# A scratch write cut at row 32 instead of row 22, and the last step's gate in halves

## The chip, the core and the metric

The kernel runs on one core of a Trainium2 chip. The core has TensorE (PE in the profile, with PEld for its weight loads), VectorE (DVE), ScalarE (ACT), GpSimd (POOL) and SyncE (SP), which only issues DMAs; ACT issues DMAs too. The metric is the device time of one execution in microseconds. The kernel before took 2562.18 us in the median of three runs, from 2557.64 to 2562.96. The profiled execution took 2562.1 us.

## The reference

An FFT filter along the sequence, followed by a two-layer block with the gate h·cos(h):

```python
X = np.fft.rfft(x, axis=1)                    # x: (8, 3008, 256)
Y = X * (filt_r + 1j * filt_i)[None, :, :]
y = np.fft.irfft(Y, n=3008, axis=1)           # reshaped to 24064 tokens of 256
h = y @ w_in                                  # (256, 2048)
g = h * np.cos(h)
out = g @ w_out                               # (2048, 256)
```

x and the filters are float32; the two weight matrices arrive as float64.

## The kernel before

The length 3008 = 47·64 is transformed with small matrix products. A batch goes through stage 1 (47 points), stages 2 and 3 (64 points forward, filter, 64 points back) and stage 4 (47 points back). Between the stages the data lie in scratch tensors in device memory: z1 after stage 1, z2 after stage 3. Stage 4 works by **units** of five columns of 47 points each (the third has one, the last two have three); it loads a unit from z2 (line 425), multiplies it (line 435) and writes the split result y (lines 442 to 452). A **chunk** is 512 tokens, and there are 47; the first chunk needs units 0 to 2, which cover rows 0 to 21 of a batch's part of z2 when two rows of 24 values are counted per column.

The block runs over **steps** (c, s): chunk c, and slice s of eight slices of the 2048 hidden values, 376 steps in all. `hidden` makes 12 matmuls into a two-bank tile `hp` (line 466), `gate` turns it into h·cos(h), split into a high part `gh` and a low part `gl` (lines 476 to 483), and `project`, which runs two steps later, makes 12 matmuls into two accumulators (line 495). After slice 7 each accumulator is scaled on ACT and written out (lines 503 and 504). `hp` has two buffers, so step k+2 waits until the gate of step k has read its tile. Matrices and data in products of this kind are kept as a high and a low part and multiplied three times.

The first batch has its own code. `first23` writes each of its 12 pieces of z2 (128 rows of 2 KB) in two DMAs: the first n0 rows at once from ACT (line 409), which is all that the first chunk waits for, and the rest later from SP (line 412). n0 is twice the first column that chunk 0 doesn't need, 22, so that the two DMAs carry 22 and 106 rows.

The weights are loaded as pairs of 32-bit words and converted on the chip (`prep_w`, lines 222 to 239): a DMA from SP into one of three `raw` buffers, two operations on ACT, a shift on DVE (line 234), an addition on POOL, and the split on ACT and POOL. Sixteen such pieces exist, called w_in and w_out 0 to 7 in what follows; nine are converted before the steps begin, and the other seven among the steps of chunk 0. A scheduler puts each engine's instructions into one fixed order per engine, guided by its own estimate of the time of each instruction; SP's DMAs are issued in their fixed order too, and each engine waits at an instruction until what it needs is there.

Of the kernel before, what the change touches and what calls it, by code (L numbers as in the profile page):

```python
# [10 lines left out]
F32 = mybir.dt.float32  # L11
F32R = mybir.dt.float32r
I32 = mybir.dt.int32
AF = mybir.ActivationFunctionType
ALU = mybir.AluOpType
# [6 lines left out]
P = 128  # L22
NJ = NB // 2
TJ = 2 * NA
TC = 512
NC = B * S // TC
NDT = D // P
NFT = DFF // P
TWO_PI = 2.0 * math.pi
# [109 lines left out]
def _units():  # L139


    sizes = [5, 5, 1] + [5] * 99 + [3, 3]
    assert sum(sizes) == B * NB
    starts = np.concatenate([[0], np.cumsum(sizes)])
    return [(int(a), int(n)) for a, n in zip(starts, sizes)]
# [10 lines left out]
def fft_filter_then_cos_glu(ctx: ExitStack, tc: tile.TileContext, ins, outT):  # L156
    nc = tc.nc
# [35 lines left out]
    NS = NFT // 2  # L193
# [4 lines left out]
    units = _units()  # L198
# [4 lines left out]
    n_first = len(of_chunk[0])  # L203
# [57 lines left out]
    def psum_f(b):  # L261
        if b == 0 and len(done) < n_first:
            if not spare:
                spare.extend(ps_h.tile([P, 2, 512], F32, name="hp")[:, u] for u in range(2))
                spare.append(ps_f.tile([P, 512], F32, name="ps", tag="ps"))
            return spare.pop(0)
        return ps_f.tile([P, 512], F32, name="ps", tag="ps")
# [115 lines left out]
    def first23(i, fas, fbs):  # L383
        cols = slice(512 * i, 512 * i + 512)
        zf = fft.tile([P, 512], F32, name="zf", tag="ld", bufs=5)
        nc.sync.dma_start(zf, z1s[0].rearrange("j (h c k) d -> (j h c) (k d)", h=2, c=2)[:, cols])
        yield
        ps = psum_f(0)
        nc.tensor.matmul(ps, mats["f2"], zf, start=True, stop=True)
        half = slice(2 * (i % 2), 2 * (i % 2) + 2)  # L390
        ya = fft.tile([P, 512], F32, name="ya", bufs=2)
        yb = fft.tile([P, 512], F32, name="yb", tag="sw", bufs=2)
        for y, f in ((ya, fas), (yb, fbs)):
            nc.vector.tensor_tensor(y, ps, f[i // 2][:, half].rearrange("p k d -> p (k d)"), ALU.mult)
        yield
        ps = psum_f(0)
        if i == 0:
            for m, c in (("30", slice(0, D)), ("3", slice(D, 512))):
                nc.tensor.matmul(ps[:, c], mats["f" + m], ya[:, c], start=True, stop=False)
                nc.tensor.matmul(ps[:, c], mats["f" + m + "i"], yb[:, c], start=False, stop=True)  # L400
        else:
            nc.tensor.matmul(ps, mats["f3"], ya, start=True, stop=False)
            nc.tensor.matmul(ps, mats["f3i"], yb, start=False, stop=True)
        tag, bufs = at2[i]
        z = fft.tile([P, 512], F32, name="z2t", tag=tag, bufs=bufs)
        nc.scalar.copy(z, ps)
        to = z2[:NJ].rearrange("j (h c k) d -> (j h c) (k d)", h=2, c=2)[:, cols]
        n0 = 2 * units[n_first][0]
        nc.scalar.dma_start(to[:n0], z[:n0])
        yield  # L410
        wrote2.setdefault(0, []).append(i)
        nc.sync.dma_start(to[n0:], z[n0:])  # L412
# [43 lines left out]
    gs, accs = {}, {}  # L456

    def hidden(c, s):
        yh, yl = ys[c]
        assert of_chunk[c] <= done  # L460
        hp = ps_h.tile([P, 2, 512], F32, name="hp")
        for u in range(2):
            fs = slice(u * P, (u + 1) * P)
            for t in range(NDT):
                for n, (w, y) in enumerate(((0, yh), (0, yl), (1, yh))):
                    nc.tensor.matmul(hp[:, u], w_in[s][w][:, t, fs], y[:, t],  # L466
                                     start=(t == 0 and n == 0), stop=(t == NDT - 1 and n == 2))
                if u == 0 or t == 0:
                    yield
        with tc.high_priority() if c == 0 else nullcontext():  # L470
            gs[c, s] = gate(hp)

    def gate(h):

        g = moe.tile([P, 2, TC], F32, name="g")
        nc.vector.tensor_scalar(g, h, 0.25, MAGIC, ALU.add, ALU.add)  # L476
        nc.vector.scalar_tensor_tensor(g, g, MAGIC, h, ALU.subtract, ALU.subtract)  # L477
        nc.scalar.activation(g, g, AF.Sin, bias=half_pi, scale=-TWO_PI)  # L478
        nc.vector.tensor_tensor(g, g, h, ALU.mult)  # L479
        gh = moe.tile([P, 2, TC], F32R, name="gh")  # L480
        nc.scalar.copy(gh, g)  # L481
        gl = moe.tile([P, 2, TC], F32R, name="gl")
        nc.gpsimd.tensor_tensor(gl, g, gh.bitcast(F32), ALU.subtract)  # L483
        return gh, gl

    def project(c, s):
        if s == 0:
            accs[c] = [ps_o.tile([P, 512], F32, name=f"acc{e}") for e in range(2)]
        gh, gl = gs.pop((c, s))
        for e in range(2):  # L490
            acc = accs[c][e]
            es = slice(e * P, (e + 1) * P)
            for u in range(2):
                for n, (w, g) in enumerate(((0, gh), (1, gh), (0, gl))):
                    nc.tensor.matmul(acc, w_out[s][w][:, u, es], g[:, u],  # L495
                                     start=(s == 0 and u == 0 and n == 0),
                                     stop=(s == NFT // 2 - 1 and u == 1 and n == 2))
                if e == 0 or u == 0:
                    yield
        if s == NFT // 2 - 1:  # L500
            for e in range(2):
                o = moe.tile([P, TC], F32, name="o")
                nc.scalar.activation(o, accs[c][e], AF.Copy, scale=TWO_PI)
                nc.scalar.dma_start(outT[e * P : (e + 1) * P, TC * c : TC * (c + 1)], o)
            del accs[c], ys[c]


# [17 lines left out]
    with tc.tile_pool(name="first", bufs=12) as first, tc.manual_schedule(engines={mybir.EngineType.SP}):  # L525
        fas, fbs, load, sign = filters(first)
        ones = [first1(i, first) for i in range(NJ // 4)]
        twos = [first23(i, fas, fbs) for i in range(n23)]
        for g in ones:
            next(g)  # L530
# [6 lines left out]
        for what in "fzzfzzfzfzzfzzfwzwzwzwwww":  # L537
# [5 lines left out]
            else:  # L543
                g = prep.pop(0)(first if len(raws) < 4 else None)
# [15 lines left out]
    moe = ctx.enter_context(tc.tile_pool(name="moe", bufs=2, reuse_waits="tile"))  # L560
# [23 lines left out]
    last = [-1000]  # L584
# [20 lines left out]
    for b in range(1, B):  # L605
# [5 lines left out]
        for i in range(n1):  # L611
            t = start + step * (2 * i + 1)
            plan(stage1(b, i), t - AHEAD1, [t, t + step])
        for i in range(n23):
            t = start + step * (2 * n1 + 2 * i + 2) + GAP12
# [6 lines left out]
    for k in range(len(steps) + LAG):  # L622
        parts = []
        if k < len(steps):
            c, s = steps[k]
            if c == 0:
                while prep and len(prep) > 2 * (NS - 1 - s) - JUST_W:
                    convert()
            parts.append(hidden(c, s))
        if k >= LAG:  # L630
            parts.append(project(*steps[k - LAG]))
        now = SLOTS * k
        for g in parts:
            for _ in range(SLOTS // 2):
                run_due(now)
                next(g, None)
                now += 1
# [52 lines left out]
```

## Time and profile before

| | |
|---|---|
| median of three runs | 2562.18 us |
| profiled execution | 2562.1 us |
| its span, first to last instruction | 2560.3 us |
| PE busy | 2455.7 us, 96% |
| DVE, ACT, POOL busy | 74%, 50%, 56% |
| mean granted clock of TensorE | 0.979 |

All times inside the execution count from the start of the span. What lies outside the span is 1.8 us. A row of the timeline or of a group names the engine, the line of the program, the operation, what is written from what, and the busy time. A queue's row (SPq, ACTq) is the issue of a DMA, not its transfer. "DMA share" is the mean busy share of the core's 16 DMA engines. The bracket behind a row, or the part behind the second bar, is the time for which the engine stood idle before it, and the instruction or DMA that ended it.

### The profile page before, as it was taken

To read this page: it belongs to the slowest core of one execution; us is meant where nothing else is said; L and a number is where in the kernel's file an instruction comes from. 1 tells how busy PE (TensorE), PEld (TensorE's weight loads), DVE (VectorE), ACT (ScalarE), POOL (GpSimd) and SP (SyncE) were. 2 spreads that over 40 slices of the span, in tenths; PEclk is the share of its full clock that TensorE was granted. 3 is DMA by queue.
4 is the path that set the end of the run, shared out by engine and by line. 5 is a ranking of instruction groups with operands and counts; after the bars stand their busy time and mean duration, and the time that the engine had idled before them with its cause. 6 is when DMAs were issued, how large, how long until landed. Compare 5 with 4: busy or idle time off the path is not lost.

```text
span 2560.3 us, 29873 instructions
## 1 busy us (share of the span) xinstructions
PE 2455.7 (96%) x10783; PEld 1967.7 (77%) x10783; DVE 1885.4 (74%) x1911; ACT 1286.1 (50%) x1707; POOL 1430.5 (56%) x826
## 2 busy tenths in 40 slices
PE   7369889999999999999999999999999999999999
PEld 2257767888888888888888888888888888888887
DVE  2177987888678877888668886787768886666665
ACT  1355564555545555555545555455554554444443
POOL 1366664656656565656546665566555554444443
PEclk8679999999999999999999999999999999999999
DMA  9253342322322232222313223222312211000000
GB/s 318 72 166 89 129 144 65 119 82 82 85 83 91 90 91 71 93 90 78 93 47 105 86 85 85 79 94 74 100 43 88 99 54 48 24 21 9 17 9 17
DMA packets 134749, 212.27 MB, mean 83 GB/s; under 512 B 12521, under 2 KB 64281, under 8 KB 134601
## 3 DMA queue, kind: packets, MB, share of 16 engines
q1 hardware_dynamic: 82385, 137.97, 17.7%
q10 hardware_dynamic: 52216, 72.39, 8.8%
q8 instruction: 86, 1.41, 0.2%
q14 instruction: 62, 0.51, 0.1%
HBM read 135.33 MB, written 74.97 MB: 82 GB/s over the span
## 4 chain that ended last, share of the span: by engine, by line
PE 82%; DVE 7%; DMA 3%; issue 3%; SPq 2%; ACT 2%; POOL 1%; POOLq 0%; ACTq 0%; DVEq 0%
PE hp L466 36%; PE acc L495 36%; PE ps L435 3%; PE ps L251 2%; PE ps L252 2%; PE ps L253 2%; SPq L412 2%; DVE g L476 1%; DMA xf<-in_x 1%; DVE sw L325 1%; DVE g L477 1%; DMA raw<-in_w_in 1%; ACT g L478 1%; DVE g L479 1%; DVE xo L280 1%
## 5 line engine op out<-in xcount | busy, mean ns | idle before, releaser
L483 POOL TENSOR_TENSOR gl<-g,gh 128x1024 fp32r<-128x1024 f32 x376 | 910.7, 2422 | 825.6 <-ACT gh L481 510.7
L466 PE MATMUL hp<-y,w_in 128*128 128x512 f32 x4512 | 1132.6, 400 | 65.8 <-DVE g L479 63.8
L466 PEld LDWEIGHTS hp<-y,w_in 128*128 128x128 f32 x4512 | 845.3, 190 | 266.6 <-issue 59.8
L495 PE MATMUL acc<-gh,w_out 128*128 128x512 f32 x3008 | 896.9, 396 | 0.7 <-ACT gh L481 0.7
L479 DVE TENSOR_TENSOR g<-g,hp 128x1024 f32<-128x1024 f32 x376 | 457.9, 1218 | 320.6 <-ACT g L478 320.1
L478 ACT ACTIVATE g<-g,half_pi 128x1024 f32<-128x1024 f32 x376 | 433.4, 1153 | 484.2 <-DVE g L477 436.6
L495 PEld LDWEIGHTS acc<-gh,w_out 128*128 128x128 f32 x3008 | 564.0, 188 | 131.1 <-ACT gh L481 1.1
L481 ACT CAST gh<-g 128x1024 fp32r<-128x1024 f32 x376 | 394.9, 1051 | 430.5 <-DVE g L479 424.1
L476 DVE TENSOR_SCALAR g<-hp 128x1024 f32<-128x1024 f32 x376 | 458.8, 1220 | 137.7 <-PE hp L466 130.3
L495 PE MATMUL acc<-gl,w_out 128*128 128x512 f32 x1504 | 549.9, 400 | 1.3 <-POOL gl L483 1.3
L477 DVE SCALAR_TENSOR_TENSOR g<-g,hp 128x1024 f32<-128x1024 f32 x376 | 458.0, 1218 | 9.9
L495 PEld LDWEIGHTS acc<-gl,w_out 128*128 128x128 f32 x1504 | 283.7, 189 | 66.7 <-POOL gl L483 2.1
L452 POOL TENSOR_TENSOR y<-y,y 128x470 fp32r<-128x470 f32 (+29 forms) x142 | 124.9, 884 | 55.8 <-ACT y L449 55.8
L435 PEld LDWEIGHTS ps<-m,z 120*128 120x128 f32 (+1 forms) x816 | 129.3, 192 | 21.0
L314 POOL TENSOR_TENSOR zl<-zf,zh 128x512 fp32r<-128x512 f32 x84 | 111.7, 1330 | 47.8 <-DVE zh L313 24.5
L331 POOL TENSOR_TENSOR yl<-ya,yh 128x512 fp32r<-128x512 f32 x84 | 113.2, 1348 | 42.1 <-ACT yh L330 42.0
L435 PE MATMUL ps<-m,z 120*128 120x120 f32 (+1 forms) x816 | 129.2, 273 | 0.0
L325 DVE SCALAR_TENSOR_TENSOR sw<-sw,sg,f 128x256 f32<-128x256 f32 x168 | 116.9, 735 | 0.0
L313 DVE CAST zh<-zf 128x512 fp32r<-128x512 f32 x84 | 93.1, 1108 | 23.1 <-DMA zf<-z 13.4
L327 DVE TENSOR_TENSOR ya<-ya,sw 128x512 f32<-128x512 f32 x84 | 98.5, 1173 | 0.0
L330 ACT CAST yh<-ya 128x512 fp32r<-128x512 f32 x84 | 51.8, 618 | 91.0 <-DVE ya L327 90.7
L449 ACT CAST y<-y 128x470 fp32r<-128x470 f32 (+29 forms) x150 | 66.9, 456 | 41.3 <-DVE y L443 38.9
(96 smaller groups left out, 1413.3 us busy)
## 6 DMA issues: line engine op xcount, KB each, us to landing
z<-z SPq DMA_DIRECT2D x101, 240.0 KB
out_t<-o ACTq DMA_DIRECT2D x94, 256.0 KB
f<-in_fb SPq DMA_DIRECT2D x84, 256.0 KB
f<-in_fa SPq DMA_DIRECT2D x84, 256.0 KB
zf<-z SPq DMA_DIRECT2D x84, 256.0 KB
z<-z2t ACTq DMA_DIRECT2D x84, 256.0 KB
xf<-in_x SPq DMA_DIRECT2D x42, 480.0 KB
z<-z1t ACTq DMA_DIRECT2D x84, 240.0 KB
```

The lines of the kernel that those rows point to most:

```text
L325: nc.vector.scalar_tensor_tensor(sw[:, ks], sw[:, ks], sg[:, 2 * i + k : 2 * i + k + 1], fbt[:, ks], ALU.mult, ALU.mult)
L331: nc.gpsimd.tensor_tensor(yl, ya, yh.bitcast(F32), ALU.subtract)
L435: nc.tensor.matmul(v[:, t, a * r : (a + 1) * r], zf[:, a, t * P : (t + 1) * P], mats[f"m4{a}"][:r, :r], start=True, stop=True)
L452: (nc.vector if i < 2 * n_first else nc.gpsimd).tensor_tensor(yl, part, yh.bitcast(F32), ALU.subtract)
L466: nc.tensor.matmul(hp[:, u], w_in[s][w][:, t, fs], y[:, t], start=(t == 0 and n == 0), stop=(t == NDT - 1 and n == 2))
L476: nc.vector.tensor_scalar(g, h, 0.25, MAGIC, ALU.add, ALU.add)
L477: nc.vector.scalar_tensor_tensor(g, g, MAGIC, h, ALU.subtract, ALU.subtract)
L478: nc.scalar.activation(g, g, AF.Sin, bias=half_pi, scale=-TWO_PI)
L479: nc.vector.tensor_tensor(g, g, h, ALU.mult)
L481: nc.scalar.copy(gh, g)
L483: nc.gpsimd.tensor_tensor(gl, g, gh.bitcast(F32), ALU.subtract)
L495: nc.tensor.matmul(acc, w_out[s][w][:, u, es], g[:, u], start=(s == 0 and u == 0 and n == 0), stop=(s == NFT // 2 - 1 and u == 1 and n == 2))
```

## The change

There are three edits. The first sets n0 to 32, so that a piece of the first batch is written as 32 rows from ACT and 96 rows from SP. The second concerns the last of the 376 steps alone: its gate runs as two calls on 512 columns each, one behind each half of the 12 matmuls, and the subtraction that makes `gl` is on VectorE there; the other steps keep one call on 1024 columns with the subtraction on GpSimd. For that, the tiles `g`, `gh` and `gl` are now allocated ahead of the matmuls in every step. The third concerns the last accumulator of the last chunk: columns 0 to 255 are scaled on ScalarE and written from its queue as before, and columns 256 to 511 are scaled on VectorE and written from SP's queue.

```diff
@@ first23
-        n0 = 2 * units[n_first][0]
+        n0 = 32
         nc.scalar.dma_start(to[:n0], z[:n0])
         yield
         wrote2.setdefault(0, []).append(i)
         nc.sync.dma_start(to[n0:], z[n0:])
@@ hidden, gate
+        last = (c, s) == (NC - 1, NS - 1)
+        g = moe.tile([P, 2, TC], F32, name="g")
+        gs[c, s] = gh, gl = [moe.tile([P, 2, TC], F32R, name=v) for v in ("gh", "gl")]
         for u in range(2):
...
+                if last and t == NDT - 1:
+                    gate(*(v[:, u] for v in (hp, g, gh, gl)), nc.vector)
                 if u == 0 or t == 0:
                     yield
-        with tc.high_priority() if c == 0 else nullcontext():
-            gs[c, s] = gate(hp)
+        if not last:
+            with tc.high_priority() if c == 0 else nullcontext():
+                gate(hp, g, gh, gl, nc.gpsimd)
...
-        nc.gpsimd.tensor_tensor(gl, g, gh.bitcast(F32), ALU.subtract)
-        return gh, gl
+        engine.tensor_tensor(gl, g, gh.bitcast(F32), ALU.subtract)
@@ project
-                nc.scalar.activation(o, accs[c][e], AF.Copy, scale=TWO_PI)
-                nc.scalar.dma_start(outT[e * P : (e + 1) * P, TC * c : TC * (c + 1)], o)
+                n = 2 if (c, e) == (NC - 1, 1) else 1
+                for k in range(n):
+                    cols = slice(k * TC // n, (k + 1) * TC // n)
+                    to = outT[e * P : (e + 1) * P, TC * c + cols.start : TC * c + cols.stop]
+                    if k:
+                        nc.vector.tensor_scalar(o[:, cols], accs[c][e][:, cols], TWO_PI, None, ALU.mult)
+                        nc.sync.dma_start(to, o[:, cols])
+                    else:
+                        nc.scalar.activation(o[:, cols], accs[c][e][:, cols], AF.Copy, scale=TWO_PI)
+                        nc.scalar.dma_start(to, o[:, cols])
```

The scheduler's estimates change with the first edit, and so the fixed orders differ in many places of the program. Three of them follow. The first is SP's queue where the rest of the first batch is written (z_112 is z2, z2t a piece of it in SBUF, z_619 and z_624 the tiles of units 3 and 4). Before:

```order
L222 DMA raw<-in_w_out 128x2x512
L222 DMA raw<-in_w_in 128x2x512
L412 DMA z_112<-z2t 106x512 x12
L222 DMA raw<-in_w_out 128x2x512
L306 DMA f<-in_fb 128x512
L307 DMA f<-in_fa 128x512
L306 DMA f<-in_fb 128x512
L307 DMA f<-in_fa 128x512
L306 DMA f<-in_fb 128x512
L222 DMA raw<-in_w_in 128x2x512
```

Now:

```order
L222 DMA raw<-in_w_out 128x2x512
L222 DMA raw<-in_w_in 128x2x512
L412 DMA z_112<-z2t 96x512 x12
L425 DMA z_619<-z_112 120x2x256
L222 DMA raw<-in_w_out 128x2x512
L306 DMA f<-in_fb 128x512
L307 DMA f<-in_fa 128x512
L306 DMA f<-in_fb 128x512
L307 DMA f<-in_fa 128x512
L222 DMA raw<-in_w_in 128x2x512
L306 DMA f<-in_fb 128x512
L222 DMA raw<-in_w_out 128x2x512
```

The loads of w_out 3 and w_in 4, the twelve writes, and then the loads of w_out 4 and w_in 5 stand in the same sequence; the load of unit 3 has moved up between the writes and w_out 4, and that of unit 4 follows right behind the rows shown.

The second place is PE's order between steps 1 and 2 of chunk 0 (w_in_1 belongs to step 1, w_in_2 to step 2; line 466 is now line 469). Before:

```order
L466 MATMUL hp<-y_555,w_in_1_82 128x512
L466 MATMUL hp<-y_554,w_in_1_83 128x512
L466 MATMUL hp<-y_554,w_in_2_84 128x512
L466 MATMUL hp<-y_555,w_in_2_84 128x512
L466 MATMUL hp<-y_554,w_in_2_85 128x512
```

Now:

```order
L469 MATMUL hp<-y_555,w_in_1_82 128x512
L469 MATMUL hp<-y_554,w_in_1_83 128x512
L435 MATMUL ps<-m_310,z_619 128x120
L435 MATMUL ps<-m_312,z_619 128x120
L435 MATMUL ps<-m_310,z_619 128x120
L435 MATMUL ps<-m_312,z_619 128x120
L435 MATMUL ps<-m_310,z_624 128x120
L435 MATMUL ps<-m_312,z_624 128x120
L435 MATMUL ps<-m_310,z_624 128x120
L469 MATMUL hp<-y_554,w_in_2_84 128x512
L469 MATMUL hp<-y_555,w_in_2_84 128x512
L469 MATMUL hp<-y_554,w_in_2_85 128x512
```

Seven matmuls of units 3 and 4, which followed step 2 before, now stand ahead of it.

The third place is PE's order at the end of the program (w_in_7 belongs to the last step, w_out_5 and w_out_6 to the projections of the two steps before it). Before:

```order
L466 MATMUL hp<-y_18812,w_in_7_94 128x512
L466 MATMUL hp<-y_18811,w_in_7_95 128x512
L495 MATMUL acc_19275<-gh,w_out_5_106 128x512
L495 MATMUL acc_19275<-gh,w_out_5_107 128x512
L495 MATMUL acc_19276<-gh,w_out_5_106 128x512
```

Now:

```order
L497 MATMUL acc_19275<-gh,w_out_6_108 128x512
L497 MATMUL acc_19275<-gh,w_out_6_109 128x512
L497 MATMUL acc_19276<-gh,w_out_6_108 128x512
L497 MATMUL acc_19276<-gh,w_out_6_109 128x512
L469 MATMUL hp<-y_18814,w_in_7_94 128x512
L469 MATMUL hp<-y_18815,w_in_7_94 128x512
L469 MATMUL hp<-y_18814,w_in_7_95 128x512
L469 MATMUL hp<-y_18814,w_in_7_94 128x512
L469 MATMUL hp<-y_18815,w_in_7_94 128x512
L469 MATMUL hp<-y_18814,w_in_7_95 128x512
L497 MATMUL acc_19275<-gl,w_out_6_108 128x512
```

Of the last step's 12 matmuls the first six stand where they were, ahead of the projection with w_out_5, and the last six have moved behind that projection and the first four matmuls of the next.

More of the change, by code (lines that the diff above doesn't have):

```diff
@@ L467, in hidden, with gate @@
                                      start=(t == 0 and n == 0), stop=(t == NDT - 1 and n == 2))
+                if last and t == NDT - 1:
+                    gate(*(v[:, u] for v in (hp, g, gh, gl)), nc.vector)
                 if u == 0 or t == 0:
                     yield
-        with tc.high_priority() if c == 0 else nullcontext():
-            gs[c, s] = gate(hp)
-    def gate(h):
-        g = moe.tile([P, 2, TC], F32, name="g")
+        if not last:
+            with tc.high_priority() if c == 0 else nullcontext():
+                gate(hp, g, gh, gl, nc.gpsimd)
+    def gate(h, g, gh, gl, engine):
         nc.vector.tensor_scalar(g, h, 0.25, MAGIC, ALU.add, ALU.add)
@@ L479, in gate @@
         nc.vector.tensor_tensor(g, g, h, ALU.mult)
-        gh = moe.tile([P, 2, TC], F32R, name="gh")
         nc.scalar.copy(gh, g)
-        gl = moe.tile([P, 2, TC], F32R, name="gl")
-        nc.gpsimd.tensor_tensor(gl, g, gh.bitcast(F32), ALU.subtract)
-        return gh, gl
+        engine.tensor_tensor(gl, g, gh.bitcast(F32), ALU.subtract)
     def project(c, s):
```

## The prediction

> **What bounds the kernel now.** I read the groups of the page first, then the busy times by stage, then the waits of the stage that stands out. The costliest group names PE's one long idle time:
>
> ```profile
> L466 PE MATMUL hp<-y,w_in 128*128 128x512 f32 x4512 | 1132.6, 400 | 65.8 <-DVE g L479 63.8
> ```
>
> Where it lies is seen from the busy time by stage (columns: stretch, its length, busy time of PE, PEld, DVE, ACT and POOL with counts, TensorE's granted clock, DMA share, GB/s):
>
> ```profile
> 87.00:96.00 9.00, 8.27 (x24) 6.21 (x24) 1.18 (x4) 3.88 (x8) 5.05 (x4) 0.69 0.13 51
> 96.00:137.00 41.00, 0.00 (x0) 0.00 (x0) 0.00 (x0) 0.45 (x1) 0.00 (x0) 0.54 0.29 106
> 137.00:200.00 63.00, 50.32 (x205) 39.47 (x206) 54.23 (x54) 37.38 (x59) 48.72 (x29) 0.86 0.51 139
> 200.00:330.00 130.00, 122.92 (x540) 97.86 (x539) 108.52 (x113) 70.44 (x102) 83.17 (x52) 0.97 0.37 113
> 330.00:500.00 170.00, 160.86 (x705) 128.54 (x704) 136.76 (x138) 88.25 (x123) 104.67 (x63) 0.98 0.35 104
> 500.00:2300.00 1800.00, 1798.65 (x8078) 1463.69 (x8077) 1391.62 (x1411) 948.76 (x1248) 1043.27 (x601) 1.00 0.25 78
> ```
>
> From 500 us on PE has no idle time worth a name. From 96 to 137 us no engine works at all. So whatever shortens that hole shifts everything behind it by as much, because all engines stand still in it together. The waits between 85 and 200 us (total, times, longest) give its chain:
>
> ```profile
> PE hp L466 <- DVE g L479: 51.8, 4, 48.2
> DVE t L234 <- ACT o L231: 47.4, 2, 47.0
> ACT o L231 <- DMA raw<-in_w_out: 44.6, 2, 44.1
> ```
>
> Step 2's matmuls wait for the gate of step 0 to release `hp`; that gate stands behind a weight conversion in DVE's fixed order; the conversion waits on ACT for the load of w_out 4. That load stands in SP's queue behind the twelve writes of line 412:
>
> ```profile
> 77.97 0.40 SPq L222 DMA_DIRECT2D raw<-in_w_out  x1
> 78.62 0.40 SPq L222 DMA_DIRECT2D raw<-in_w_in  x1
> 79.06 43.36 SPq L412 DMA_DIRECT2D z<-z2t  x12
> 122.52 4.30 SPq L222 DMA_DIRECT2D raw<-in_w_out  x1
> ```
>
> And while the writes run, the DMA engines are nearly empty:
>
> ```profile
> 40.00:64.00 24.00, 20.92 (x48) 8.57 (x46) 9.71 (x16) 5.08 (x9) 7.84 (x5) 1.00 1.04 395
> 83.00:122.00 39.00, 10.59 (x35) 8.20 (x33) 3.51 (x10) 5.56 (x13) 7.58 (x6) 0.59 0.13 52
> ```
>
> A share of 0.13 of 16 engines is two engines (2/16 = 0.125), at some 25 GB/s each, where the same core moved 395 GB/s from 40 to 64 us. One write of 106 rows of 2 KB is 217 kB, so at 52 GB/s it takes 4.2 us, and twelve take 50 us. The hole is 106 rows going through two engines.
>
> **Part 1: 96 rows instead of 106.** The question is over how many engines 96 rows go. The nearest row is the first batch's input, 96 rows of 2 KB, which was alone in the queue from 5 to 7 us:
>
> ```profile
> xf<-in_x SPq DMA_DIRECT2D x4, 192.0 KB
> 5.00:7.00 2.00, 2.00 (x4) 0.75 (x3) 0.69 (x1) 0.00 (x0) 0.00 (x0) 1.00 1.00 303
> ```
>
> With 96 rows the share is 1.00, at 303 GB/s. So a write of 197 kB costs between 0.50 us (at 395 GB/s) and 0.65 us (at 303), and twelve cost 6.0 to 7.8 us in place of 50.
>
> [...]
>
> What is late next? The queue's order behind 78 us is: w_out 3 and w_in 4 (1.05 MB), the twelve writes (2.36), unit 3 (0.25), w_out 4 (0.52), four filter loads (1.05), w_in 5 (0.52), a filter load (0.26), w_out 5 (0.52), unit 4 (0.25). The instructions at both ends of the hole:
>
> ```profile
> 87.29 8.27 PE L466 MATMUL hp<-y,w_in 128*128 128x512 f32 x24 [1.97 <-ACT y L449]
> 91.79 0.62 ACT L238 CAST w_in<-o 128x512 fp32r<-128x512 f32 x1 [1.26 <-POOL o L235]
> 136.55 0.66 ACT L231 ACTIVATE o<-raw 128x512 f32<-128x512 f32 x1 [44.14 <-DMA raw<-in_w_out]
> 137.66 1.22 DVE L476 TENSOR_SCALAR g<-hp 128x1024 f32<-128x1024 f32 x1
> 142.44 1.21 DVE L479 TENSOR_TENSOR g<-g,hp 128x1024 f32<-128x1024 f32 x1
> 143.80 4.58 PE L466 MATMUL hp<-y,w_in 128*128 128x512 f32 x12 [48.24 <-DVE g L479]
> ```
>
> Up to and with w_out 4 it is 4.18 MB, from about 78.5 us: 10.6 us at 395 GB/s, 13.8 at 303, so the last byte at 89.1 to 92.3. For issue and receipt I add 2.2 us (an estimate: the last output DMA, below, is issued at 2557.43 and the span ends at 2560.3; less 0.7 us for its 262 kB). W_out 4 is then there at 91.3 to 94.5. ACT is not free for it before 92.41 (91.79 + 0.62). From ACT's start to the first gate DVE took 1.11 us (136.55 to 137.66), so that gate starts at 93.5 to 95.6, and step 2, which followed 6.14 us later (137.66 to 143.80), at 99.7 to 101.7. Step 1's matmuls, done at 95.56, are early enough, since DVE turns to them 2.5 us after it begins.
>
> The moved order adds a wait of its own: matmuls of unit 4 now stand ahead of step 2, so PE can't begin step 2 before unit 4's load lands. That is 6.78 MB after 78.5 us: at 395 GB/s 95.7 + 2.2 = 97.9, at 303 GB/s 103.1. Behind it on PE stands step 2, and for that the gates of DVE. So step 2 starts at 99.7 to 103.1; I take 101, between the gate's and the load's ends: **42.8 us** earlier, with bounds 40.7 and 44.1. The seven matmuls themselves lie in PE's idle time.
>
> The ten rows more per piece that ACT writes are 12 × 20 kB = 0.25 MB, 0.6 us at 395 GB/s, spread over DMAs of 42 to 75 us while the filters and weights load. I take nothing; at worst 0.6 us.
>
> **Part 2: the last step.** The end before:
>
> ```profile
> 2541.53 2.96 PE L466 MATMUL hp<-y,w_in 128*128 128x512 f32 x12
> 2542.76 1.22 DVE L479 TENSOR_TENSOR g<-g,hp 128x1024 f32<-128x1024 f32 x1 [1.28 <-ACT g L478]
> 2544.07 1.05 ACT L481 CAST gh<-g 128x1024 fp32r<-128x1024 f32 x1 [1.34 <-DVE g L479]
> 2550.85 2.36 POOL L483 TENSOR_TENSOR gl<-g,gh 128x1024 fp32r<-128x1024 f32 x1 [3.19 <-ACT gh L481]
> 2553.26 3.52 PE acc L495 x8
> 2557.43 0.34 ACTq L504 DMA_DIRECT2D out_t<-o  x1
> ```
>
> PE waits for `gl`, then runs the last eight matmuls in 3.52 us, 0.44 each, where twelve take 2.80 (0.23 each) in the steady state. Halves cost as these groups do (the third and fourth: shortest, median and longest):
>
> ```profile
> 2538.89 2.80 PE acc L495 x12
> L394 DVE TENSOR_TENSOR ya<-ps,ff 128x512 f32<-128x512 f32 x4 | 2.8, 690 | 3.0 <-PE ps L389 3.0
> L503 ACT ACTIVATE o<-acc x94: 574/597/604, 211.2 to 2556.8; 128x512 f32<-128x512 f32 x94
> L452 DVE TENSOR_TENSOR y<-y,y x8: 164/644/1731, 83.8 to 177.8; 128x470 fp32r<-128x470 f32 x4, 128x84 fp32r<-128x84 f32 x1, 128x10 fp32r<-128x10 f32 x1, 128x74 fp32r<-128x74 f32 x1
> ```
>
> With 0.6 to 0.7 us for an operation on a half and 0.1 for a hand-over: DVE is free at 2543.98 and the first half is in `hp` by then. Two operations to 2545.3, the sine to 2546.0, the product to 2546.7, `gh` at 2547.4, `gl` on DVE at 2548.1. The second half's matmuls now run after 12 + 4 others, ending near 2541.53 + 22 × 0.233 = 2546.7 plus their own 1.4 = 2548.1, just when DVE takes them up: `gh` at 2551.7, `gl` at 2552.4. PE comes to the last projection at 2549.9, does six matmuls of the first half to 2551.3, waits 0.4, and ends at 2553.2, against 2553.26 + 3.52 = 2556.78. The longest chain is then one accumulator of 0.60 us and half of the other, 0.35, both on ACT, and their two DMAs: the last issue near 2554.4 against 2557.43. **3.0 us** gained.
>
> Bounds: if `gl`'s first half takes the 1.73 us of the longest such row, the second half slips by 1.1 us, and 1.9 are left; if the first accumulator's eviction were free too, 3.6. VectorE's half of the last accumulator ends before ACT's, and gains at most the 0.3 that ACT's second operation is shorter by.
>
> **The sum.** The profiled execution took 2562.1 us, 0.1 below the median, so it stands for it. 2562.1 − 42.8 − 3.0 = 2516.3, say **2516**. The order of everything up to 500 us has changed as well. PE was idle there for 12.7 + 7.1 + 9.1 = 28.9 us behind the hole; I allow 5 us either way for how the new order falls. Its own range: 2562.1 − 44.1 − 3.6 − 5 = 2509 to 2562.1 − 40.7 − 1.9 + 5 + 0.6 = 2525.
>
> **Rivals.**
> - *The DMA engines become the bound.* Rows of the stretch behind the hole show loads of weights and units together at a lower rate:
>
> ```profile
> 139.00:149.00 10.00, 5.20 (x20) 4.34 (x20) 6.61 (x7) 7.72 (x10) 4.95 (x4) 0.59 1.06 296
> ```
>
>  The 395 GB/s of 40 to 64 us speak against it. If the queue made only 200 GB/s, unit 4 would land at 78.5 + 33.9 + 2.2 = 114.6, step 2 would gain 29, and the time would be 2530. It decides from below 330 GB/s, where the load and not the gate is last.
> - *The new order costs more than I allow.* Half of the 28.9 us idle time again, 14 us: 2530. For it speaks that the orders differ on all engines, against it that the work and its limits are the same.
> - *The writes were no cause.* Were w_out 4 late for another reason, only the end would gain: 2559. Against it: the load's issue starts at 122.52, right behind the writes.
> - *Slower: the early tiles.* `g`, `gh` and `gl` are allocated ahead of the matmuls in all 376 steps. If that moved a wait for a free buffer onto PE, each step would pay; from 45.8 / 376 = 0.12 us a step it eats the gain, and at 0.15 us the time is 2572. Against it: the tiles' first writers and their order within a step are the same as before, and PE had 1.4 us idle in 1800 us.
>
> **Chances.** The forecast 0.80, the DMA bound 0.08, the order 0.06, no cause 0.03, slower 0.03. A change of under 0.2% (5.1 us) can't be told from none here. Faster by more: 0.80 + 0.08 + 0.06 = 0.94; within 0.2%: 0.03; slower: 0.03. The range for 8 in 10 and the neighbouring cases: 2504 to 2532.
>
> **What would show it.** The issues of line 412 take some 5 to 8 us together in place of 43.36, at a DMA share near 1; DVE's first gate starts at 93.5 to 95.6 and step 2 at 99.7 to 103.1, with PE's wait of 48.24 us down to 4 to 7, ended by a gate or by unit 4's load; no PE wait on POOL at the end, and the last DMA issue 3 us nearer to the last whole step. It is wrong if twelve writes of 96 rows still show a share near 0.13, or if step 2 begins on time and the gain is gone by 500 us.

## The result, and the profile after

The changed kernel took 2517.57 us in the median of four runs (2515.22 to 2520.8), the kernel before 2561.74 (four runs, 2557.64 to 2562.96). The ratio is 0.9831, with a 95% interval from 0.9814 to 0.9848. The forecast was 2516, with 2504 to 2532 as its range. One execution of e6 below took 3367.65 us at a granted clock of 0.665 and is left out of its row.

The profiled execution has a span of 2515.5 us in place of 2560.3. Three marks in PE's timeline divide the 44.8 us: the start of step 2 of chunk 0, and the first matmul of the last step.

| | before | after | difference |
|---|---|---|---|
| up to step 2 | 143.80 | 102.94 | −40.9 |
| step 2 to the last step | 2397.7 | 2396.2 | −1.6 |
| last step to the end of the span | 18.77 | 16.40 | −2.4 |

SP's queue after, from its timeline (start, time of the issue, line):

```profile
78.73 0.40 SPq L222 DMA_DIRECT2D raw<-in_w_in  x1
79.17 8.77 SPq L412 DMA_DIRECT2D z<-z2t  x12
88.04 0.59 SPq L425 DMA_DIRECT2D z<-z  x1
88.73 0.58 SPq L222 DMA_DIRECT2D raw<-in_w_out  x1
...
94.38 2.34 SPq L425 DMA_DIRECT2D z<-z  x4
```

The twelve writes take 8.77 us to issue, where they took 43.36, and while they run the DMA share is 1.02, at 377 GB/s. The busy time by stage (columns as in the prediction, the last three the granted clock, the DMA share and GB/s):

```profile
82.00:88.00 6.00, 3.76 (x16) 3.33 (x16) 3.31 (x10) 3.06 (x9) 3.54 (x3) 0.50 1.02 377
96.00:103.00 7.00, 1.67 (x10) 1.49 (x9) 6.93 (x9) 5.60 (x9) 2.67 (x3) 0.73 1.09 327
```

The hole that is left is short, and on PE it is ended by the load of unit 4. PE's timeline, and ACT's and DVE's at the same place:

```profile
95.27 1.05 PE L435 MATMUL ps<-m,z 120*128 120x120 f32 x8
101.64 1.64 PE L435 MATMUL ps<-m,z 120*128 120x120 f32 x6 [5.33 <-DMA z<-z]
102.94 1.63 PE L469 MATMUL hp<-y,w_in 128*128 128x512 f32 x3
94.40 0.67 ACT L231 ACTIVATE o<-raw 128x512 f32<-128x512 f32 x1 [1.98 <-DMA raw<-in_w_out]
95.51 1.22 DVE L481 TENSOR_SCALAR g<-hp 128x1024 f32<-128x1024 f32 x1
100.29 1.22 DVE L484 TENSOR_TENSOR g<-g,hp 128x1024 f32<-128x1024 f32 x1
```

The last six rows of PE, ACT, DVE and SP:

```profile
2509.77 1.19 PE L497 MATMUL acc<-gh,w_out 128*128 128x512 f32 x4 [0.37 <-ACT gh L485]
2510.80 0.63 PE L497 MATMUL acc<-gl,w_out 128*128 128x512 f32 x2
2511.24 0.87 ACT L514 ACTIVATE o<-acc 128x512 f32<-128x512 f32 x2 [1.51 <-PE acc L497]
2511.86 0.82 ACTq L515 DMA_DIRECT2D out_t<-o  x2
2512.14 0.42 DVE L511 TENSOR_SCALAR o<-acc 128x256 f32<-128x256 f32 x1 [1.70 <-ACT o L514]
2512.59 0.36 SPq L512 DMA_DIRECT2D out_t<-o  x1
```

PE no longer waits for `gl`. But VectorE's half of the last accumulator starts only when ScalarE's half has ended, and its DMA is the last of all.

### The profile page after: what moved, and what is told of

Read it like the earlier page. It is cut to its first block, busy times and chain, and to the rows that moved or that the text cites. A ratio compares the mean times of both kernels' runs of the same rounds, so it can differ in the third digit from the quotient of the medians.

```text
span 2515.5 us, 29899 instructions
## 1 busy us (share of the span) xinstructions
PE 2454.9 (98%) x10783; PEld 1967.7 (78%) x10783; DVE 1889.6 (75%) x1917; ACT 1286.4 (51%) x1709; POOL 1426.9 (57%) x825
## 4 chain that ended last, share of the span: by engine, by line
PE 85%; DVE 7%; DMA 3%; issue 2%; ACT 2%; POOL 1%; SPq 0%; ACTq 0%; DVEq 0%; POOLq 0%
PE hp L469 38%; PE acc L497 37%; PE ps L435 3%; PE ps L251 2%; PE ps L252 2%; PE ps L253 2%; DVE g L481 1%; DVE sw L325 1%; DVE g L482 1%; DVE g L484 1%; DMA xf<-in_x 1%; ACT g L483 1%; DVE xo L280 1%; DMA zf<-z 0%; PE hp L378 0%
## 5 line engine op out<-in xcount | busy, mean ns | idle before, releaser
L452 POOL TENSOR_TENSOR y<-y,y 128x470 fp32r<-128x470 f32 (+29 forms) x142 | 127.1, 899 | 42.9 <-ACT y L449 42.8
L313 DVE CAST zh<-zf 128x512 fp32r<-128x512 f32 x84 | 86.2, 1026 | 29.8 <-DMA zf<-z 18.2
L280 DVE TENSOR_TENSOR xo<-xf 120x512 f32<-120x512 f32 (+1 forms) x49 | 55.0, 1123 | 40.9 <-DMA xf<-in_x 40.8
```

The costliest lines, as they stand in the source:

```text
L452: (nc.vector if i < 2 * n_first else nc.gpsimd).tensor_tensor(yl, part, yh.bitcast(F32), ALU.subtract)
```

## The experiments

Two theories stood against each other for the hole. Theory A: the number of a DMA's rows sets how many of the 16 DMA engines it keeps busy, and 106 rows keep two busy (a share of 0.13). Theory B: it is something else that n0 moves, the ten rows that went into the first DMA, the place of the cut, or the new fixed order. Other runs part the change into its edits, and ask why the stretch behind step 2 isn't the same in all versions. The kernel before ran beside each round of experiments, at 2558.9 to 2559.7 us in the median.

This table has them all; the times of e8, e9 and e10 are of a single run each, those of e3 and e5 of two. "Step 2", "middle" and "end" are the three parts of the span, read as above.

| run | us | ratio to before, 95% | step 2 | middle | end |
|---|---|---|---|---|---|
| before | 2561.74 | | 143.80 | 2397.7 | 18.77 |
| after | 2517.57 | 0.9831, 0.9814 to 0.9848 | 102.94 | 2396.2 | 16.40 |
| e1 first edit alone | 2516.69 | 0.9834, 0.9820 to 0.9849 | 101.19 | 2394.6 | 17.55 |
| e2 other edits alone | 2558.55 | 0.9998, 0.9989 to 1.0008 | 144.77 | 2396.6 | 16.38 |
| e3 103 rows | 2594.34 | 1.0137, 1.0117 to 1.0157 | 190.32 | 2385.3 | 16.37 |
| e4 96 and 10 rows | 2509.48 | 0.9807, 0.9791 to 0.9824 | 101.46 | 2387.9 | 17.61 |
| e5 100 rows | 2516.49 | 0.9831, 0.9812 to 0.9851 | 103.16 | 2394.2 | 16.36 |
| e6 pieces whole | 2517.75 | 0.9837, 0.9820 to 0.9853 | 108.71 | 2389.7 | 16.51 |
| e7 last five whole | 2504.16 | 0.9788, 0.9772 to 0.9805 | 99.64 | 2384.3 | 16.91 |
| e8 one eviction | 2515.55 | | 102.87 | 2394.6 | 16.35 |
| e9 gl on GpSimd | 2517.67 | | 105.25 | 2393.8 | 16.90 |
| e10 own tile | 2514.87 | | 102.69 | 2394.0 | 16.37 |
| e11 FIRST = 64 | 2515.64 | 0.9830, 0.9814 to 0.9847 | 103.47 | 2394.7 | 16.32 |
| e12 e7, one eviction | 2504.30 | 0.9786, 0.9771 to 0.9801 | 101.16 | 2384.3 | 16.73 |

### The edits apart

```diff
 # e1: the kernel before
-        n0 = 2 * units[n_first][0]
+        n0 = 32
```

> The kernel before with n0 = 32 and nothing else. Theory A (the hole is 106 rows going through two DMA engines): the twelve writes take about 9 us as in the changed kernel, step 2 starts at 101 to 103 us in place of 143.80, the end from the last step's first matmul to the end of the span stays at 18.8 us, and the time is 2519 to 2521. Rival (the ends and the early tiles carry a large part of the gain): the time stays above 2530.

```diff
 # e2: the changed kernel
-        n0 = 32
+        n0 = 2 * units[n_first][0]
```

> The changed kernel with the first batch's rows written as 22 and 106 again, so only the last step's gate, the last eviction and the early allocation of the tiles are changed. Theory A: the hole stays, step 2 starts at 143 to 145 us, the stretch from the last step's first matmul to the end of the span is 16.4 us in place of 18.8, and the time is 2.4 us shorter, 2559 to 2560. Rival (the early tiles put a wait into each step): the time grows by more than 5 us, or PE shows idle time from 500 us on.

The first edit alone has the whole measurable gain, 2516.69 us. The other two, with the early tiles, are not told from no change: 0.9998. E1 came out 2 us below what was expected for it, because its end and its middle are shorter. So the rival of the early tiles falls, and so does the one that gives the ends a large part.

In the traces the end is shorter by 2.4 us with them (18.77 to 16.38). But e1, which has the old end, took 17.55, and e4, which has it too, 17.61. The same code ran 1.2 us faster there, and the clock is what differs. The end in two stretches, of the kernel before:

```profile
2550.00:2553.00 3.00, 1.28 (x5) 0.67 (x4) 0.00 (x0) 0.72 (x1) 2.15 (x1) 1.00 0.01 3
2553.00:2557.00 4.00, 3.50 (x8) 2.26 (x8) 0.00 (x0) 0.79 (x2) 0.21 (x1) 0.58 0.11 44
```

and of e1:

```profile
2504.20:2507.20 3.00, 1.32 (x5) 0.67 (x4) 0.00 (x0) 0.73 (x1) 2.14 (x1) 1.00 0.01 3
2507.20:2511.20 4.00, 2.14 (x8) 1.42 (x8) 0.00 (x0) 1.19 (x2) 0.23 (x1) 1.00 0.17 66
```

PE is idle for nearly the same time in the first stretch of both (1.72 and 1.68 us), yet the last eight matmuls took 3.50 us at a clock of 0.58, and 2.14 at 1.00. So of the 2.4 us some 1.2 are a fall of the clock that doesn't come in each execution, and 1.2 are the edits. Why the clock fell in one and not in the other is taken up in the last section.

### The number of rows

```diff
 # e3: the changed kernel
-        n0 = 32
+        n0 = 25
```

> The changed kernel with n0 = 25: 25 rows from ACT and 103 from SP, a prime number. [...] Rival B (fewer rows, or the row at which the cut lies, or the new fixed order made the gain): a time within 10 us of the changed kernel, 2508 to 2528. Rival C (a count that is no multiple of 16 goes over two engines): 2557 to 2562.

```diff
 # e4: the kernel before; 106 rows as before, in two DMAs
-        nc.sync.dma_start(to[n0:], z[n0:])
+        nc.sync.dma_start(to[32:], z[32:])
+        nc.sync.dma_start(to[n0:32], z[n0:32])
```

> The kernel before, with the rest of each piece, 106 rows as before, written from SP in two DMAs of 96 and 10 rows: the same bytes from the same queue, twelve issues more. [...] Rival B (the ten rows that went into the first DMA, and with them the earlier load of unit 3, made the gain): step 2 still waits until after 130 us, and the time is above 2550.

```diff
 # e5: the changed kernel
-        n0 = 32
+        n0 = 28
```

> The changed kernel with n0 = 28: 28 rows from ACT and 100 from SP. [...] Rival (a count that is no multiple of 16 goes over two engines): 49 us, step 2 after 140, 2555 to 2562.

The stretch in which the writes run, of e3, of e5, and of e4:

```profile
90.00:160.00 70.00, 4.56 (x18) 3.30 (x17) 0.04 (x1) 0.85 (x2) 3.77 (x3) 0.55 0.07 26
```
```profile
84.00:90.00 6.00, 3.71 (x12) 3.10 (x12) 2.93 (x10) 3.39 (x10) 2.89 (x2) 0.50 0.66 253
```
```profile
79.00:91.00 12.00, 9.31 (x33) 8.20 (x34) 4.65 (x13) 7.10 (x16) 7.73 (x7) 0.50 0.92 294
```

Rows and share go together at four counts, as theory A has it: 103 rows at a share of 0.07 and 26 GB/s, 106 at 0.13 and 52, 100 at 0.66 and 253, 96 at 1.02 and 377. Sixteen times the share is 1.1, 2.1, 10.6 and 16.3, from which I estimate one engine, two, about ten and all. What another count would get isn't shown by these four. None of the rivals has both 103 rows slower than 106 and 100 nearly as fast as 96. In e3 most of the issues take as long as a transfer:

```profile
L412 SPq DMA_DIRECT2D z<-z2t x12: 323/8202/8210, 79.0 to 157.9; - x12
```

8.2 us for 211 kB is 25.7 GB/s. Step 2 starts at 190.32, and the time, 2594.34, lies outside what both rivals allowed. With three rows fewer than before, in the same kind of queue, the kernel is 35 us slower.

E4 moves no row into the first DMA and still loses the hole: the same 106 rows, cut into 96 and 10, go at a share of 0.92 and 294 GB/s. So neither the moved rows nor the earlier load of unit 3 made the gain. Nor did the fixed order: in e5 SP has the order of the kernel before behind the writes (w_out 4, then filters, units 3 and 4 later), and the hole is gone there too. Theory B has no part left that a run supports.

E5, which writes 100 rows at a share of 0.66, is as fast as the changed kernel, but not because the lower share costs nothing. Its writes are issued in 10.87 us in place of 8.77, and w_out 4 and the gate of step 0 come 1.5 us later:

```profile
95.92 0.66 ACT L231 ACTIVATE o<-raw 128x512 f32<-128x512 f32 x1 [5.31 <-DMA raw<-in_w_out]
101.80 1.21 DVE L484 TENSOR_TENSOR g<-g,hp 128x1024 f32<-128x1024 f32 x1
103.16 5.46 PE L469 MATMUL hp<-y,w_in 128*128 128x512 f32 x12 [7.76 <-DVE g L484]
```

In its order no matmul of unit 4 stands ahead of step 2. Those take 1.3 us in the changed kernel, and so step 2 starts only 0.2 us later here.

In e3 and e4 the middle is 10 to 12 us shorter than in the kernel before, 2385.3 and 2387.9 us against 2397.7, and their times, 2594 and 2509, are lower by as much than their step 2 alone would make them.

### What sets the middle

In 2 us stretches over the 360 us behind step 2 I added up the time for which PE is idle, and the clock that is lost (length times one minus the granted clock):

| run | PE idle | clock lost | sum | middle less the sum |
|---|---|---|---|---|
| before | 22.0 | 11.9 | 33.9 | 2363.8 |
| after | 21.9 | 11.7 | 33.6 | 2362.6 |
| e1 | 21.6 | 11.5 | 33.1 | 2361.5 |
| e2 | 20.6 | 12.9 | 33.5 | 2363.1 |
| e3 | 15.7 | 4.8 | 20.5 | 2364.8 |
| e4 | 20.8 | 5.7 | 26.5 | 2361.4 |
| e5 | 18.7 | 11.5 | 30.2 | 2364.0 |
| e6 | 19.1 | 8.3 | 27.4 | 2362.3 |
| e7 | 19.7 | 1.7 | 21.4 | 2362.9 |
| e8 | 24.3 | 8.3 | 32.6 | 2362.0 |
| e9 | 25.0 | 7.6 | 32.6 | 2361.2 |
| e10 | 22.8 | 10.8 | 33.6 | 2360.4 |
| e11 | 25.4 | 6.3 | 31.7 | 2363.0 |
| e12 | 18.9 | 3.4 | 22.3 | 2362.0 |

The middles spread over 13.5 us, what is left without the sum over 4.4. The lost clock counts idle time as well; counted only where PE is busy it is 0.1 to 2.0 us less, and then the spread of what is left is 3.3. So these two account for most of the difference, and between the changed kernel and e7 nearly all of it is clock: 11.7 us lost against 1.7, at nearly the same idle time. The row of the 360 us for the changed kernel, and for e7:

```profile
102.94:462.94 360.00, 338.18 (x1458) 268.20 (x1458) 303.32 (x299) 193.24 (x278) 234.73 (x142) 0.97 0.37 110
```
```profile
99.64:459.64 360.00, 340.28 (x1491) 269.33 (x1492) 298.92 (x307) 199.67 (x286) 238.49 (x144) 1.00 0.39 114
```

One fall of the clock in the changed kernel:

```profile
131.00:133.00 2.00, 0.49 (x1) 0.18 (x1) 2.00 (x3) 1.25 (x2) 2.00 (x3) 1.00 0.39 41
133.00:135.00 2.00, 0.85 (x2) 0.76 (x3) 2.00 (x2) 1.95 (x3) 2.00 (x2) 0.57 0.96 279
135.00:139.00 4.00, 4.00 (x10) 3.04 (x10) 4.00 (x3) 2.67 (x4) 3.07 (x3) 0.50 0.75 209
139.00:141.00 2.00, 2.00 (x8) 1.63 (x7) 2.00 (x2) 1.14 (x2) 2.00 (x1) 0.72 0.00 0
```

PE is busy for 1.34 of the 4 us from 131 to 135. The clock falls at 133.3, while PE is still waiting, and stays at half until 140.1. PE goes on at 134.15 and is busy from there, so behind the 2.7 us of waiting some 3.0 us more are lost (half of 6.0).

To see whether an order alone moves the middle, one constant of the planner was moved:

```diff
 # e11: the changed kernel
-FIRST, LENGTH, BEFORE = 60, 376, 160
+FIRST, LENGTH, BEFORE = 64, 376, 160
```

> The changed kernel with one planner constant moved, FIRST from 60 to 64: the second batch's first stage enters the program four slots later. It removes no work and touches neither the writes nor the end. Theory E (the 2384 to 2398 us between step 2 and the last step follow the fixed order, through PE's idle time and the clock that falls behind it): step 2 within 2 us of 102.94, the end within 0.3 us of 16.4, and the stretch between differs from 2396.2 by several us, by about as much as PE's idle time and the loss of clock differ together. Rival (that stretch is shorter only where the writes changed): within 2 us of 2396.2.

The middle came out at 2394.7, 1.5 us from 2396.2: inside the 2 us of the rival. PE was idle 3.5 us longer and lost 5.4 us less clock. Together that is 1.9 us less, near the 1.5 measured, but so small a shift of the middle doesn't show what theory E says; that the fixed order, rather than the arrival of data, decides how often the clock falls at PE's waits, stays open.

### A better version

```diff
 # e6: the changed kernel, each piece in one DMA from ACT
-        n0 = 32
+        n0 = P
-        nc.sync.dma_start(to[n0:], z[n0:])
```

> The changed kernel with each piece of the first batch written whole, 128 rows in one DMA from ACT, and nothing from SP. If the writes behind 79 us are what still delays unit 4 and w_out 4 in the changed kernel (PE waits 5.33 us for unit 4, DVE 4.83 for w_out 4), that wait goes: 2.36 MB less in the queue is 6 to 8 us, so step 2 starts as soon as the gate lets it, at 97 to 100. Against that the seven pieces written before 64 us add 1.4 MB where the DMA share is 1.04: 3.5 us later filters and weights, and step 0 up to 3.5 us later than 87.30. Together -5 to +3 us. If the rest of the program follows its fixed order by chance, the stretch behind step 2 differs by up to 10 us, as it does between the runs so far (2401.7 to 2416.5 us).

```diff
 # e7: the changed kernel, the last five pieces in one DMA from ACT
-        n0 = 32
+        n0 = 32 if i < 7 else P
-        nc.sync.dma_start(to[n0:], z[n0:])
+        if n0 < P:
+            nc.sync.dma_start(to[n0:], z[n0:])
```

> As the run before, but only the last five pieces are written whole from ACT, in the stretch from 66 to 78 us where the DMA share is 0.07 to 0.37; the first seven keep 32 rows from ACT and 96 from SP. Expected: step 0 at 87 to 88 as in the changed kernel, 1 MB less behind 79 us, unit 4 and w_out 4 some 3 us earlier, step 2 at 99 to 101, the time 0 to 4 us shorter, plus what the order behind it does.

```diff
 # e12: e7 without the third edit
-                n = 2 if (c, e) == (NC - 1, 1) else 1
+                n = 1
```

> The version with the last five pieces written whole from ACT, 2504.16 us, without the third edit. Expected: the same time within 3 us, 2501 to 2507; step 2 at 99 to 100, the end 16.2 to 16.5 us. If the third edit matters, the end is 0.3 us or more longer.

E7 and e12 beat both kernels, at 2504.2 and 2504.3 us. From 66 to 78 us the DMA engines go from a share of 0.19 to 0.35, and carry 1 MB there that would have waited; the first row is of the changed kernel, the second of e7:

```profile
66.00:78.00 12.00, 6.75 (x13) 2.53 (x11) 5.05 (x8) 10.42 (x21) 10.13 (x8) 0.78 0.19 46
```
```profile
66.00:78.00 12.00, 4.75 (x10) 1.68 (x10) 4.69 (x6) 10.39 (x21) 10.57 (x9) 0.92 0.35 117
```

Step 0 begins at 87.30 in both, and step 2 at 99.64 in e7, 3.3 us earlier, waiting for the gate and no longer for a unit:

```profile
99.64 3.07 PE L470 MATMUL hp<-y,w_in 128*128 128x512 f32 x12 [1.09 <-DVE g L485]
```

That is the part that was expected. Most of the 14.7 us in span between the two (2515.5 and 2500.8) is the middle: 11.9 us, by the clock above, which wasn't. E6 shows the other side: with all twelve pieces whole, step 0 begins at 95.10, 7.8 us late where at most 3.5 was expected, step 2 at 108.71 where 97 to 100 was, and the time is no better than that of the changed kernel. Of the 7.8 us, the larger part comes from the writes: the last of the twelve is issued at 79.45 in place of 74.89, and PE begins unit 0 at 84.50 in place of 79.46. The rest comes from the order, in which the matmuls of units 3 and 4 stand ahead of step 0 and wait for a load:

```profile
84.50 2.06 PE L434 MATMUL hp<-m,z 120*128 120x120 f32 x8 [7.36 <-DMA z<-z]
91.67 3.77 PE L434 MATMUL ps<-m,z 120*128 120x120 f32 x16 [2.57 <-DMA z<-z]
95.10 7.17 PE L468 MATMUL hp<-y,w_in 128*128 128x512 f32 x24
93.16 0.33 DVE L451 TENSOR_TENSOR y<-y,y 128x84 fp32r<-128x84 f32 x2 [0.33 <-ACT y L448]
```

ACT has the last y that step 0 needs ready at 93.2, when VectorE's row starts; in e5 step 0 begins as soon as that row does (87.36 and 87.35). So the order costs 1.9 us. Why the writes are 4.6 us late and not 3.5 isn't settled. E12 has e7's time and middle, but its step 2 (101.16) and its end (16.73) lie outside what was expected.

### The end

```diff
 # e10: the changed kernel, VectorE's half in a tile of its own
+                        o2 = moe.tile([P, 2, TC], F32, name="g")[:, 0, : TC // 2]
-                        nc.vector.tensor_scalar(o[:, cols], accs[c][e][:, cols], TWO_PI, None, ALU.mult)
-                        nc.sync.dma_start(to, o[:, cols])
+                        nc.vector.tensor_scalar(o2, accs[c][e][:, cols], TWO_PI, None, ALU.mult)
+                        nc.sync.dma_start(to, o2)
```

> The changed kernel with VectorE's half of the last accumulator written into a tile of its own. In the changed kernel VectorE starts that half only at 2512.14, after ScalarE's half of the same accumulator has ended (idle 1.70, ended by ACT L514). Theory C (it waits because both halves go to one tile): with its own tile it starts with the accumulator's last matmul, at the time at which ScalarE takes up the first accumulator, some 0.6 us earlier, and the last DMA is ScalarE's; the end is 0.2 to 0.4 us shorter. Theory D (the two reads of one accumulator are kept apart): the wait stays.

```diff
 # e8: the changed kernel
-                n = 2 if (c, e) == (NC - 1, 1) else 1
+                n = 1
```

> The changed kernel without the third edit: the last accumulator is scaled whole on ScalarE and written in one DMA. In the run with a tile of its own VectorE's half still waited for ScalarE's (idle 1.77, ended by ACT), so the two halves run one behind the other: 0.27 + 0.42 us and a hand-over in place of 0.60. If that is so, the third edit is worth nothing or less: from the last step's first matmul to the end of the span 16.2 to 16.5 us, against 16.40 in the changed kernel. If it is worth something, 16.7 or more.

```diff
 # e9: the changed kernel
-                    gate(*(v[:, u] for v in (hp, g, gh, gl)), nc.vector)
+                    gate(*(v[:, u] for v in (hp, g, gh, gl)), nc.gpsimd)
```

> The changed kernel with the last step's subtraction on GpSimd again, still in halves. A half on GpSimd takes some 1.2 us (2.36 for the whole) against 0.69 on VectorE, and frees VectorE for the second half. In the changed kernel PE waited 0.37 us for the second half's gh and not for gl. Expected: gl of the second half 0.6 us later, 0.3 us of it behind PE's matmuls on gh, so the end 0.2 to 0.5 us longer than 16.40. If VectorE is what the second half waits for, the end is the same or shorter.

With its own tile VectorE's half waits all the same:

```profile
2509.85 0.42 DVE L512 TENSOR_SCALAR g<-acc 128x256 f32<-128x256 f32 x1 [1.77 <-ACT o L515]
```

So the tile that they write isn't what keeps the two halves apart. What they still share is the accumulator that both read, as theory D has it; whether the program or the chip keeps them apart isn't shown. Run one behind the other they gain nothing: without the third edit the end is 16.35 us, with it 16.40, and in the pair e12 and e7 16.73 and 16.91. With `gl` on GpSimd a half takes longer, and the end is 0.5 us longer, 16.90:

```profile
2509.70 1.29 POOL L486 TENSOR_TENSOR gl<-g,gh 128x512 fp32r<-128x512 f32 x1 [3.25 <-ACT gh L485]
```

PE's last two matmuls start 12.04 us behind the first of the last step there, and 11.70 in the changed kernel. So 0.3 of the 0.5 us is seen on PE; the rest is within the spread of the ends, as e7 shows, which has the last step of the changed kernel and an end of 16.91. VectorE's subtraction is thus worth some 0.3 to 0.5 us, from one trace each; that the rest, about 0.7 us against e1's end, is the halves is a difference and not an experiment.

## Why the prediction was right

**The hole.** That 106 rows go through two engines was read from a share of 0.13, and no run speaks against it: e3, e4 and e5 leave none of the other readings. The cost of the writes now was put at 6.0 to 7.8 us, and the issues take 8.77, 1.0 us above the bound.

**What is late next.** W_out 4 was to arrive between 91.3 and 94.5, and ACT takes it up at 94.40. The first gate was to start at 93.5 to 95.6: 95.51. Unit 4's load, the wait that the new order adds, was to land between 97.9 and 103.1; PE goes on at 101.64. The gate of step 0 has read its tile at 101.51 (100.29 + 1.22), so the two come together, and the load is the last by 0.1 us. Step 2 starts at 102.94, inside 99.7 to 103.1 and near its late end. The term was 42.8 us and measures 40.9. Of the 1.9 us, 1.3 are the matmuls of unit 4, six rows between the load and step 2. The prediction let them lie in PE's idle time, at no cost, but they stand behind the wait that ends last. The other 0.6 is the queue, which ran nearer to the slow bound.

**The end.** The term of 3.0 us measures 2.4 in the trace. Two steps of it were off. The time between the last step's first matmul and PE's last one was worked out as 11.7 us (2553.2 less 2541.53), and is 12.3 (2510.80 + 0.63 less 2499.10). Of the 0.6 us, 0.5 are there already when VectorE takes up the second half, and about half of them are a wait that the sum put at nothing. The last six matmuls of the last step write the second half of `hp`, and they begin when VectorE's product has read the first half:

```profile
2503.73 0.69 DVE L484 TENSOR_TENSOR g<-g,hp 128x512 f32<-128x512 f32 x1 [0.85 <-ACT g L483]
2504.48 1.66 PE L469 MATMUL hp<-y,w_in 128*128 128x512 f32 x6
2506.18 0.69 DVE L481 TENSOR_SCALAR g<-hp 128x512 f32<-128x512 f32 x1 [0.32 <-PE hp L469]
```

They start 5.4 us behind the step's first matmul where 5.1 was counted, and VectorE takes the second half up after 7.1 us where the sum had 6.6. Whether the program or the chip holds them back isn't shown. From there to `gh` it takes 3.6 us, as worked out: the operations on halves, 0.62 to 0.72 us, were priced rightly. And "VectorE's half of the last accumulator ends before ACT's" is wrong: it starts behind it. That cost nothing that shows, since the last DMA is issued 1.2 us after PE's end, as in the sum. Moreover the old end's 0.44 us per matmul, which made half of the gain, was taken as part of the old code. It was the clock of that execution, 0.58 there; e1 has the same code at 1.00, with 0.27 us per matmul.

**The sum** came out within 2 us, 2516 against 2517.57, and that closely by luck: two terms too large by 2.5 us together were partly made up for by a middle that is 1.6 us shorter, and 1.2 of the 2.4 us at the end are the clock. The main term and its cause were right without luck. The 5 us that I allowed for the order were enough here, but not for the kind of change: in the runs the middle lies anywhere between 2384 and 2398 us.

**The rivals.** The DMA engines as the bound: the queue is what comes last, 0.1 us behind the gate, at 327 to 377 GB/s; the prediction had the two meet at 330. No cause, and slower by the early tiles: e1 and e2 speak against both.

## What to carry to other kernels

A DMA share that sat at a sixteenth or an eighth for tens of microseconds (0.07 and 0.13), with issues that took 4 to 8 us each, came here from writes of 103 and 106 rows. Cutting the rows at 96, even as one more DMA, was enough (shares of 1.02 and 0.92), and with 100 rows at 0.66 the kernel took the same time, 2516.49 us against 2517.57. What stood in the queue behind the slow DMAs paid for them: the load of w_out 4 was issued at 122.52 us in place of 88.73, and all engines stood still for it. A matmul that the order puts ahead of a waiting step isn't free because PE is idle there; the six of unit 4 cost 1.3 us, since the wait in front of them was the last to end. And before an end or a wait is priced from one trace, its granted clock has to be read: the same eight matmuls took 3.50 us in one execution and 2.14 in another.

## What the hardware showed

Waits of the same length came with a fall of TensorE's clock in one execution and not in another. In the 360 us behind step 2 of all 14 kernels the clock is either 1.00 or 0.50, and each of the 44 times that it falls there it stays at half for 3.41 or 6.83 us; its changes there in one execution lie on one grid of 3.41 us. Cut at that grid, the kernel before shows this at its end:

```profile
2550.21:2553.62 3.41, 1.54 (x6) 0.98 (x7) 0.00 (x0) 0.51 (x1) 2.36 (x1) 1.00 0.01 2
2553.62:2557.03 3.41, 3.15 (x8) 1.95 (x6) 0.00 (x0) 0.82 (x2) 0.00 (x0) 0.50 0.13 52
```

and e1, behind the same two waits of 0.7 and 1.3 us:

```profile
2503.35:2506.77 3.42, 2.17 (x9) 1.10 (x7) 0.45 (x1) 1.05 (x1) 1.71 (x1) 1.00 0.01 2
2506.77:2510.18 3.41, 2.14 (x8) 1.42 (x8) 0.00 (x0) 0.98 (x2) 0.66 (x1) 1.00 0.00 0
```

In the kernel before nearly all of both waits lies in one stretch of the grid, in which PE is busy for 1.54 us, and the next is at half; in e1 they are spread over two, with 2.17 and 2.14, and the clock stays at 1.00. From step 2 on, the traces of the kernel before and of the changed kernel show the clock fall after each of the eight stretches at full clock in which PE was busy for 0.68 to 1.43 us, after two of the four with 1.53 to 1.59, and after none with 1.91 or more. So where the waits fell on the grid fits with whether the clock fell; what makes it fall isn't shown. In the 360 us of the 14 traces between 1.7 and 12.9 us of clock were lost, besides the 16 to 25 for which PE was idle.
